# Sparse attention into a Swish MLP: batch 2's first transposes, batch 1's norms, and the later score and AV groups take other places in the order

## The chip, the cores and the metric

One core of a Trainium2 chip runs the whole kernel. The metric is device time in microseconds (us), the median of several runs. The engines of the core work side by side, each through its own list of instructions in order: TensorE (PE in the profile) does matmuls, VectorE (DVE) and ScalarE (ACT) do element-wise work, GpSimd (POOL) and SyncE (SP) here mostly send DMAs. An engine that reaches an instruction whose input is not ready waits, and so does all that is behind it on that engine.

## The reference

Four batches of eight heads, 768 tokens, head size 64. Each query sees the keys within 16 positions of it, and besides them 24 block summaries: the maximum of the keys, and the mean of the values, of each block of 32 tokens. The heads' outputs side by side are the 512 features of a token, and these go through a two-layer MLP with Swish.

```python
k_sum = k.reshape(B, H, nb, block, D).max(axis=3)
v_sum = v.reshape(B, H, nb, block, D).mean(axis=3)
scores_l = scale * np.matmul(q, k.transpose(0, 1, 3, 2))      # kept where |i - j| < 16
scores_s = scale * np.einsum('bhsd,bhnd->bhsn', q, k_sum) + np.log(block)
a = softmax over [scores_l | scores_s]
attn_out = np.matmul(a, concat([v, v_sum]))                   # -> x (3072 x 512)
h = x @ w_in                                                  # 512 -> 2048
out = (h * sigmoid(beta * h)) @ w_out                         # 2048 -> 512
```

## The kernel before, in words

The heads of a batch are taken two at a time, so a batch has four pairs, 0 to 3. For a pair:

- GpSimd loads v, k and q as bf16 (`load_next`, with lines 111, 118, 124 and 126). In the trace the loaded tiles are ve, k_nat and q_nat.
- `copy_v` (line 328) makes a second, shifted copy of v, vo, with two DMAs on SP. `cross` (lines 303 and 305) turns k and q by two transposing DMAs on SP, into kw and qt. For batch 0 and half of batch 1 TensorE turns them instead, and for two pairs of batch 1 ScalarE copies v.
- `max_k` (lines 311 and 313; `top_k`, line 293, in batch 1) takes the key maxima of the blocks on VectorE, and `rows_k` (lines 319 and 320) puts them beside the keys. `mean_v` (line 340 on TensorE, 347 on VectorE) and `rows_v` (line 353) do the same for the means of v.
- `scores` (line 438) is done for two pairs at once: 144 small matmuls in three groups, each followed by ScalarE's exponential (line 440). `mask` (line 447, VectorE) clears what is outside the window, one instruction for a pair.
- `av` (line 464) multiplies by v on TensorE, `norm` (lines 473 and 474, VectorE) divides by the sums and leaves x_nat, and `x_transpose` turns it into xT: by a transposing DMA on SP (line 483), or for batch 0 and pairs 2 and 3 of batch 1 by TensorE (line 488).

For a batch's MLP, 16 "h groups" (line 509 on TensorE, then ScalarE's Silu, line 516) make the hidden layer, and 24 "o parts" of four matmuls each (line 530) the output. Four o parts are 128 tokens: then ScalarE copies the result to o_sb, of which there are three buffers (line 550), and SP stores it (line 551). I number these stores 0 to 5 within a batch.

The order of all this is written out by hand. The loop over b (line 637) works on batch b's MLP and, in its gaps, on batch b+1's attention; I call its rounds stage 0, 1, 2 and 3. The MLP steps form the list `main`, with times in a planner's own unit: an h group counts 1.3, an o part 0.865, and `up` (20.8) is where the o parts begin. The attention steps are put into the list `side` by `at_time(t, ...)`, and each is issued just ahead of the first step of `main` whose time is not below t. So the numbers in the code are places in an order, the same for every engine's queue, and not times on the chip. In stage 0 an `open_gate` step lets GpSimd begin batch 2's loads; batch 3's loads are steps of stage 1. At the end of a stage come two steps of the next stage's MLP on three quarters of its input, which need xT of pairs 0, 1 and 2; the next stage then begins with the last quarter, pair 3.

Of the kernel before, what the change touches and what calls it, by code (L numbers as in the profile page):

```python
# [12 lines left out]
def kernel(  # L13
# [94 lines left out]
    def load_row(nm, b, g):  # L108
        t = qk_pool.tile([P, nch, 2, D], bf16, name=nm + "_nat", tag=nm + "_row")
        for h in range(2):  # L110
            nc.gpsimd.dma_start(out=t[:, :, h], in_=(k_row if nm == "k" else q_row)[b, g, :, h])  # L111
        nat[(nm, b, g)] = t

    def load_v(b, g, n=1):
        lo, hi = PC * g + 1, min(PC * (g + n) + 1, HC)
        rows = v[b].rearrange("h s d -> (h s) d")
        src = rows[lo * P - W:hi * P - W].rearrange("(c p) d -> p c d", p=P)
        nc.gpsimd.dma_start(out=ve_bufs[b % 2][:, lo:hi, 0:D], in_=src)  # L118

    def load_v_edge(b, last):  # L120
        ve = ve_bufs[b % 2]
        rows = v[b].rearrange("h s d -> (h s) d")
        if last:
            nc.gpsimd.dma_start(out=ve[0:W, HC, 0:D], in_=rows[H * S - W:H * S])
        else:
            nc.gpsimd.dma_start(out=ve[W:P, 0, 0:D], in_=rows[0:P - W])
# [370 lines left out]
    def h_group(u, i, ks=range(k1)):  # L497

        b, t0, w = units[u]
        nn = 2 // w  # L500
        if 0 in ks:
            if (i * nn) % (k2 // w) == 0:
                h_bufs[(u, i * nn * w // k2)] = moe_pool.tile([P, k2 // w, w * MG], bf16, name="h_sb", tag="h_sb", bufs=4)
            h_open[(u, i)] = ps.tile([P, 2, 512], f32, name="h_ps", tag="big", bufs=3)
        big = h_open[(u, i)]
        for j in range(2):
            ni, tok = (i, t0 + j * MG) if w == 2 else (2 * i + j, t0)
            for ki in ks:
                nc.tensor.matmul(big[:, j, 0:MG], w_in_sb[:, ki, ni * P:(ni + 1) * P], xT[b][:, ki, tok:tok + MG],  # L509
                                 start=(ki == 0), stop=(ki == k1 - 1))  # L510
        if k1 - 1 not in ks:
            return
        for j in range(nn):
            ni = i * nn + j
            hb = h_bufs[(u, ni * w // k2)][:, ni % (k2 // w)]
            nc.scalar.activation(out=hb.rearrange("p (k m) -> p k m", m=MG), in_=big[:, j:j + w, 0:MG],  # L516
                                 func=ACTF.Silu, scale=beta_sb[:, ni:ni + 1])
# [119 lines left out]
    for b in range(B):  # L637
        us = [u for u, z in enumerate(units) if z[0] == b]
        up = sum(NG[u] for u in us) * GT
        total = up + nch * 4 * OT  # L640
        nxt = b + 1 if b + 1 < B else None
        pairs = tuple(range(npair))
        side = []

        def at_time(t, f, *a):
            side.append((t, lambda: f(*a)))

        if b == 0:
            for g in pairs:
                t = 3.9 if g < 2 else 6.5  # L650
                at_time(0.6 + 1.3 * g, mask_half, g)
                at_time(0.6 + 1.3 * g, rows_v, 0, g, HM, nch)
                if g % 2 == 0:
                    at_time(t, av_pair, g)
                at_time(t, norm, (0, g, 1), HM)
                at_time(t + 2.6, x_transpose, (0, g, 1), HM, HM, "t", dve)
            at_time(7.0, fill_band, 0, HM)
            at_time(7.0, band_edge, False)
            for n in range(k2):
                at_time(up - 7.5 + 0.4 * n, scale_w_out, n)  # L660
        if nxt == 1:
            for g in pairs:
                if g < 2:
                    p = up - 9.0 + 4.5 * g
                    at_time(p, prep_k, 1, g, "t")
                    at_time(p, prep_q, 1, g, "t", dve)
                    at_time(p + 0.8, copy_v, 1, g)
                else:
                    p = (up + 6.1, up + 7.8)[g - 2]
                    at_time(up + 0.5, cross, 1, g)  # L670
                    at_time((up + 4.0, up + 6.1)[g - 2], copy_v, 1, g, 0, nch, act)
                at_time(p, top_k, 1, g)
                at_time(p, rows_k, 1, g)
            at_time(up + 3.4, mean_v, 1, pairs, "big")
            for g0, t, r, a, xt in ((0, up + 0.3, up + 3.4, up + 7.7, 0.1), (2, up + 12.9, up + 12.9, up + 17.2, 2.6)):
                at_time(t, scores, 1, g0)
                for f in (rows_v, mask):
                    for g in (g0, g0 + 1):
                        at_time(r, f, 1, g)
                for g in (g0, g0 + 1):  # L680
                    at_time(a, av, (1, g), 0, nch)
                for g in (g0, g0 + 1):
                    at_time(a, norm, (1, g), nch)
                    at_time(a + xt, x_transpose, (1, g), 0, nch, "big", dve)
        elif nxt is not None:
            for g in pairs:

                at_time(0.1 + 0.2 * g, copy_v, nxt, g)
                at_time(0.2 + 0.2 * g, cross, nxt, g)
                m = 3.9 + 3.9 * g if g < 2 else up + 1.0  # L690
                at_time(m, max_k, nxt, g)
                at_time(m, rows_k, nxt, g)
            at_time(14.0, mean_v, nxt, pairs)
            for g in pairs:
                at_time(14.1 + 1.0 * g, rows_v, nxt, g)
            for g0, t, a in ((0, up + 0.8, up + 5.9), (2, up + 9.0, up + 14.5)):
                at_time(t, scores, nxt, g0)
                for g in (g0, g0 + 1):
                    at_time(t, mask, nxt, g)
                    at_time(a, av, (nxt, g), 0, nch)  # L700
                for g in (g0, g0 + 1):
                    at_time(a, norm, (nxt, g), nch)
                    at_time(a, x_transpose, (nxt, g), 0, nch, "big", dve)
        if nxt is not None:
            if nxt + 1 < B:
                def load_next(b, g):
                    if g == 0:
                        nc.gpsimd.memset(ve_bufs[b % 2][SUM:P, 0:HC, D:VW], 1.0)
                        load_v_edge(b, False)
                    load_v(b, g)  # L710
                    if g == npair - 1:
                        load_v_edge(b, True)
                    load_row("k", b, g)
                    load_row("q", b, g)

                def open_gate():

                    nc.vector.memset(gate[:], 0.0)
                    nc.gpsimd.memset(gate[:], 0.0)

                if b == 0:
                    at_time(up + 6.0, open_gate)
                for g in pairs:
                    at_time(up + 6.0 + 0.01 * (g + 1) if b == 0 else 8.0 + 3.5 * g, load_next, nxt + 1, g)
        main = []
        for j, u in enumerate(us):
            for i in range(NG[u]):
                ks = range(k1 - 1, k1) if j == 0 and i < 2 else range(k1)
                main.append(((j * NG[u] + i) * GT, lambda u=u, i=i, ks=ks: h_group(u, i, ks)))
        for j, u in enumerate(us):  # L730
            n = units[u][2] * HM
            main += [(up + (4 * (j * n + ms) + p) * OT, lambda u=u, ms=ms, p=p: o_part(u, ms, p, 4)) for ms in range(n) for p in range(4)]
        if nxt is not None:
            main += [(total + i, lambda i=i: h_group(us[-1] + 1, i, range(k1 - 1))) for i in range(2)]
        side.sort(key=lambda z: z[0])
        for t, f in main:
            while side and side[0][0] <= t:
                side.pop(0)[1]()
            f()
        for _, f in side:  # L740
            f()
# [30 lines left out]
```

## Time and profile before

| | us |
|---|---|
| median of 3 runs (214.22 to 215.84) | 214.43 |
| the profiled execution, its own time | 214.58 |
| its span, first to last instruction | 212.9 |
| TensorE busy | 202.8 |
| ScalarE busy | 116.7 |
| VectorE busy | 87.8 |
| GpSimd busy | 66.8 |

TensorE's granted clock is 0.997 of full speed over the span. Busy times overlap, since the engines run side by side. The DMA engines are busy from the start to about 130 us, and much less after that.

How to read the rows that follow. A timeline row gives start, duration, engine, line, operation, what is written and read, and how many instructions were merged; in brackets stands how long the engine had been idle before, and what ended that. SPq is SP's queue, whose rows last as long as SP is occupied with sending. A DMA's "landing" is counted from the start of its sending until its data has arrived. A row of waits has the waiting work, what it waited for, and then the sum, the number and the longest. A row of the page's groups ends in busy us, mean ns of one, and idle time ahead of it. Matmuls overlap, so the mean duration of one is longer than its share of the busy time.

### The profile page before, as it was taken

Reading aid. Unit: us, or ns where it says so; the run is one execution under the profiler, and the core shown is the slowest. Engines: PE = TensorE matmul, PEld = TensorE weight load, DVE = VectorE, ACT = ScalarE, POOL = GpSimd, SP = SyncE. Lnnn points to the kernel's source line nnn. Section 1 sums busy time; section 2 is a strip of 40 time slices with the busy share of each in tenths; the row PEclk is TensorE's granted clock in tenths of the full one; section 3 lists DMA queues with packets and bytes.
Section 4 is the critical chain, followed back from the end, with each engine's and each line's share of the span. In section 5 each row is a group of like instructions: output and inputs, shape, how many; then the busy total and the mean of one; then the engine's idle time right before and its main releaser. Section 6 shows DMA issues by size and latency. Waiting matters only on the chain.

```text
span 212.9 us, 4838 instructions
## 1 busy us (share of the span) xinstructions
PE 202.8 (95%) x2005; PEld 113.6 (53%) x2024; DVE 87.8 (41%) x219; ACT 116.7 (55%) x159; POOL 66.8 (31%) x90
## 2 busy tenths in 40 slices
PE   7999999999989999999999799999999999999992
PEld 2656666655545565555455355555455565554452
DVE  4677891882795502164834005313834000002121
ACT  3799668889635186668161366668162476630000
POOL 7984344353399555555391000000000000000000
PEclk9999999999999999999999999999999999999998
DMA  6999999999999999999999999700153400001222
GB/s 174 174 156 188 205 204 206 186 179 168 155 156 188 235 192 169 158 123 161 144 155 145 199 229 180 139 3 0 64 161 98 127 0 3 0 2 59 89 89 62
DMA packets 93622, 28.34 MB, mean 133 GB/s; under 512 B 82256, under 2 KB 90656, under 8 KB 93600
## 3 DMA queue, kind: packets, MB, share of 16 engines
q0 software_dynamic: 63184, 13.24, 78.3%
q1 hardware_dynamic: 29968, 14.26, 35.8%
q10 hardware_dynamic: 448, 0.52, 0.7%
q8 instruction: 16, 0.26, 0.6%
q14 instruction: 6, 0.05, 0.1%
HBM read 27.27 MB, written 6.29 MB: 158 GB/s over the span
## 4 chain that ended last, share of the span: by engine, by line
PE 84%; DMA 9%; issue 2%; DVE 2%; ACT 1%; SPq 0%; POOL 0%; POOLq 0%
PE h_ps L509 39%; PE o_ps L530 33%; DMA xT<-x_nat 4%; DMA qt<-q_nat 3%; DMA q_run<-in_q_dram 3%; PE av_ps L464 2%; PE s_ps L438 2%; PE vm_ps L340 1%; PE px L488 1%; DVE x_nat L474 1%; PE pq L279 1%; PE pk L279 1%; PE s_ps L383 1%; PE av_ps L411 1%; PE s_ps L378 1%
## 5 line engine op out<-in xcount | busy, mean ns | idle before, releaser
L509 PE MATMUL h_ps<-xT,w_in_sb 128*128 128x384 bf16 x512 | 85.9, 326 | 1.6 <-DMA xT<-x_nat 1.5
L530 PE MATMUL o_ps<-w_out_sb,h_sb 128*128 128x512 bf16 (+2 forms) x383 | 82.9, 370 | 2.0 <-issue 1.6
L516 ACT ACTIVATE h_sb<-h_ps,beta_sb 128x768 bf16<-128x768 f32 (+1 forms) x80 | 59.3, 772 | 25.1 <-PE h_ps L509 25.0
L509 PEld LDWEIGHTS <-w_in_sb 128*128 128x128 bf16 x512 | 49.2, 98 | 35.0 <-issue 2.1
L530 PEld LDWEIGHTS <-h_sb 128*128 128x128 bf16 x400 | 37.5, 98 | 41.6
L550 ACT COPY o_sb<-o_ps 128x512 f32<-128x512 f32 x18 | 10.7, 592 | 33.2 <-PE o_ps L530 16.8
L111 POOL DMA_DIRECT2D k_nat<-in_k_dram x20 | 16.8, 842 | 15.5 <-DMA ve<-in_v_dram 5.7
L440 ACT ACTIVATE attn<-s_ps 128x1024 bf16<-128x1024 f32 x18 | 17.2, 1024 | 7.2 <-PE s_ps L438 7.1
L111 POOL DMA_DIRECT2D q_nat<-in_q_dram x20 | 16.8, 847 | 9.9 <-DMA ve<-in_v_dram 6.5
L550 DVE COPY o_sb<-o_ps 128x512 f32<-128x512 f32 x5 | 3.5, 692 | 39.5 <-PE o_ps L530 39.5
L447 DVE TENSOR_TENSOR attn<-attn,band 128x1536 bf16<-128x1536 bf16 x12 | 11.2, 957 | 13.9 <-ACT attn L440 13.8
L118 POOL DMA_DIRECT2D ve<-in_v_dram x12 | 14.3, 1191 | 7.0 <-DMA w_in_sb<-in_moe_w_in_dram 2.7
L474 DVE TENSOR_TENSOR x_nat<-av_ps,r 128x768 bf16<-128x768 f32 (+1 forms) x20 | 16.0, 798 | 0.7
L311 DVE TENSOR_TENSOR half<-kw 128x384 bf16<-128x384 bf16 x8 | 2.8, 355 | 28.2 <-DMA kw<-k_nat 28.2
L293 DVE TENSOR_REDUCE km<-kw 128x24 bf16<-128x768 bf16 x8 | 7.6, 948 | 2.4 <-DMA kw<-k_nat 1.3
L473 DVE RECIPROCAL r<-av_ps 128x12 f32<-128x12 f32 (+1 forms) x20 | 4.2, 212 | 8.3 <-PE av_ps L464 7.5
L464 PEld LDWEIGHTS <-attn 128*64 128x64 bf16 x336 | 6.0, 111 | 3.0 <-issue 2.4
L298 DVE COPY qt<-pq 128x768 bf16<-128x768 bf16 x5 | 4.8, 958 | 5.8 <-PE pq L279 5.8
L464 PE MATMUL av_ps<-vo,attn 128*64 128x65 bf16 x168 | 6.9, 196 | 0.0
L353 DVE COPY ve<-vm 32x780 bf16<-32x780 bf16 x12 | 4.9, 408 | 4.7 <-DMA vo<-ve 4.4
L464 PE MATMUL av_ps<-ve,attn 128*64 128x65 bf16 x168 | 6.8, 196 | 0.0
L438 PEld LDWEIGHTS <-kw 64*128 64x128 bf16 x288 | 4.7, 95 | 3.4 <-issue 2.0
(92 smaller groups left out, 142.4 us busy)
## 6 DMA issues: line engine op xcount, KB each, us to landing
out_dram<-o_sb SPq DMA_DIRECT2D x23, 256.0 KB, 4.4
w_out_sb<-in_moe_w_out_dram POOLq DMA_DIRECT2D x4, 512.0 KB, 17.5
k_nat<-in_k_dram POOLq DMA_DIRECT2D x20, 96.0 KB, 10.6
q_nat<-in_q_dram POOLq DMA_DIRECT2D x20, 96.0 KB, 10.7
w_in_sb<-in_moe_w_in_dram POOLq DMA_DIRECT2D x3, 512.0 KB, 14.4
ve<-in_v_dram POOLq DMA_DIRECT2D x6, 192.0 KB, 10.8
vo<-ve SPq DMA_DIRECT2D x10, 97.5 KB, 6.6
ve<-in_v_dram POOLq DMA_DIRECT2D x2, 384.0 KB, 12.8
```

The costliest lines, as they stand in the source:

```text
L111: nc.gpsimd.dma_start(out=t[:, :, h], in_=(k_row if nm == "k" else q_row)[b, g, :, h])
L118: nc.gpsimd.dma_start(out=ve_bufs[b % 2][:, lo:hi, 0:D], in_=src)
L293: nc.vector.tensor_reduce(out=km_of[g], in_=keys_of(b, g).rearrange("p (n f) -> p n f", f=block), op=ALU.max, axis=mybir.AxisListType.X)
L438: nc.tensor.matmul(sv[:, h, c], kw_of(b, g)[lo:lo + D, par, m, :], qt_bufs[g][lo:lo + D, m, par], start=True, stop=True)
L440: nc.scalar.activation(out=flat[:, j * n:(j + 1) * n].rearrange("p c h f -> p h c f"), in_=sv, func=ACTF.Exp, scale=scale)
L447: nc.vector.tensor_mul(out=a, in0=a, in1=band.rearrange("p r m h f -> p (r m h f)"))
L464: nc.tensor.matmul(ov[par * QT:(par + 1) * QT, h, m], a[:, par, m, h], t[:, PC * g + nch * h + m0 + m], start=True, stop=True)
L474: nc.vector.tensor_mul(out=x.rearrange("p m h d -> p h m d"), in0=ov[:, :, :, 0:D], in1=r[:, :, :, None].to_broadcast([P, 2, n, D]))
L509: nc.tensor.matmul(big[:, j, 0:MG], w_in_sb[:, ki, ni * P:(ni + 1) * P], xT[b][:, ki, tok:tok + MG], start=(ki == 0), stop=(ki == k1 - 1))
L516: nc.scalar.activation(out=hb.rearrange("p (k m) -> p k m", m=MG), in_=big[:, j:j + w, 0:MG], func=ACTF.Silu, scale=beta_sb[:, ni:ni + 1])
L530: nc.tensor.matmul(o_ps[:, c0:c1], h_bufs[(u, ni * w // k2)][:, ni % (k2 // w), ms * P:(ms + 1) * P], w_out_sb[:, ni, c0:c1], start=(ni == ...
L550: (nc.scalar.copy if u + 1 < len(units) else nc.vector.tensor_copy)(out=o_sb[:], in_=o_ps[:])
```

## The change

Nothing is computed otherwise; steps take other places in the list. With times in the planner's unit:

- Stage 0: `copy_v` and `cross` of batch 2's pairs 0 and 1, which stood first in stage 1, are issued at up+17.4 and up+19.1, which is ahead of o parts 21 and 23 (counted from 0), and so on SP between store 4 and store 5. Pairs 2 and 3 stay first in stage 1.
- Stage 0: `top_k` and `rows_k` of batch 1's pair 2 go from up+6.1 to up+7.8, that is from ahead of `norm` of pairs 0 and 1 to behind them. `av` and `norm` of its pairs 2 and 3 go from up+17.2 to up+16.4, from ahead of o part 20 to ahead of o part 19, and their `x_transpose` from part 23 to part 22.
- Stages 1 and 2: `max_k` and `rows_k` of pair 2 go from up+1.0 to 11.7 and of pair 3 from up+1.0 to 18.0, so from behind both masks of pairs 0 and 1 to ahead of them; pair 2's are now also ahead of `mean_v`, pair 3's behind the last `rows_v`.
- Stages 1 and 2: `av` and what follows it of pairs 0 and 1 go from ahead of o part 7 to ahead of part 6; `scores` of pairs 2 and 3 from part 11 to part 9; their `av`, `norm` and `x_transpose` from part 17 to part 14. On SP the last two x transposes thereby come ahead of store 3 instead of behind it.

```diff
                 else:
-                    p = (up + 6.1, up + 7.8)[g - 2]
+                    p = up + 7.8
...
-            for g0, t, r, a, xt in ((0, up + 0.3, up + 3.4, up + 7.7, 0.1), (2, up + 12.9, up + 12.9, up + 17.2, 2.6)):
+            for g0, t, r, a, xt in ((0, up + 0.3, up + 3.4, up + 7.7, 0.1), (2, up + 12.9, up + 12.9, up + 16.4, 2.6)):
...
         elif nxt is not None:
             for g in pairs:
 
-                at_time(0.1 + 0.2 * g, copy_v, nxt, g)
-                at_time(0.2 + 0.2 * g, cross, nxt, g)
-                m = 3.9 + 3.9 * g if g < 2 else up + 1.0
+                if nxt > 2 or g > 1:
+                    at_time(0.1 + 0.2 * g, copy_v, nxt, g)
+                    at_time(0.2 + 0.2 * g, cross, nxt, g)
+                m = 3.9 + 3.9 * g if g < 3 else 18.0
...
-            for g0, t, a in ((0, up + 0.8, up + 5.9), (2, up + 9.0, up + 14.5)):
+            for g0, t, a in ((0, up + 0.8, up + 5.1), (2, up + 7.7, up + 12.0)):
...
                 if b == 0:
                     at_time(up + 6.0, open_gate)
+                    for g in range(2):
+                        at_time(up + 17.4 + 1.7 * g, copy_v, 2, g)
+                        at_time(up + 17.4 + 1.7 * g, cross, 2, g)
```

## The prediction

> **What bounds the kernel now.** I read the page first, then TensorE's waits, the chain of work in order of time, and last the timelines of TensorE, VectorE and SP around the places that the diff touches.
>
> ```profile
> PE 202.8 (95%) x2005; PEld 113.6 (53%) x2024; DVE 87.8 (41%) x219; ACT 116.7 (55%) x159; POOL 66.8 (31%) x90
> ...
> L509 PE MATMUL h_ps<-xT,w_in_sb 128*128 128x384 bf16 x512 | 85.9, 326 | 1.6 <-DMA xT<-x_nat 1.5
> L530 PE MATMUL o_ps<-w_out_sb,h_sb 128*128 128x512 bf16 (+2 forms) x383 | 82.9, 370 | 2.0 <-issue 1.6
> ...
> L550 ACT COPY o_sb<-o_ps 128x512 f32<-128x512 f32 x18 | 10.7, 592 | 33.2 <-PE o_ps L530 16.8
> ```
>
> ```profile
> PE h_ps L509 <- DMA xT<-x_nat: 1.5, 1, 1.5
> PE s_ps L438 <- DMA qt<-q_nat: 0.8, 1, 0.8
> ```
>
> TensorE is busy for 95% of the span, and no matmul is added or removed. So only its idle time can change the end: the two waits above, the start before its real work begins, and the last few us. The rows give two prices. A matmul of the first layer costs 85.9 / 512 = 0.168 us of TensorE's time, one of the second 82.9 / 383 = 0.216 us, so an "o part" of four matmuls is 0.87 us.
>
> The largest wait stands at the end of the stage that works on batch 1's tokens and prepares batch 2 (stage 1, some 74 to 123 us; stage 0 is the one before it, stage 2 the one behind). From the chain, then from TensorE's timeline:
>
> ```profile
> 68.46 0.89 PE av_ps L464 x48
> ...
> 101.96 0.88 PE av_ps L464 x48
> ...
> 115.60 7.61 DMA xT<-x_nat
> ...
> 149.85 0.88 PE av_ps L464 x48
> ...
> 167.41 20.80 PE h_ps L509 x128
> ```
>
> ```profile
> 119.36 0.49 PE L509 MATMUL h_ps<-xT,w_in_sb 128*128 128x384 bf16 x2
> 121.39 4.78 PE L509 MATMUL h_ps<-xT,w_in_sb 128*128 128x384 bf16 x27 [1.54 <-DMA xT<-x_nat]
> ```
>
> After two matmuls from 119.36 the third could start at 119.70; it starts at 121.39, when pair 2's transposed x lands: 1.7 us lost. Ten more end at 121.39 + 1.68 = 123.07, and pair 3's x, landing at 115.60 + 7.61 = 123.21, lets the next go: 0.2 us (rounded up). Together **1.9 us**, all that the change can win in this place. Stage 2 ends in 167.41 with no DMA before it in the chain: nothing to win there.
>
> **The change part by part.**
>
> *Stage 0.* Batch 1's norms go ahead of pair 2's maxima, and the AV of its pairs 2 and 3 stands one o part earlier.
>
> ```profile
> 65.03 1.83 DVE L447 TENSOR_TENSOR attn<-attn,band 128x1536 bf16<-128x1536 bf16 x2
> ```
>
> VectorE does the same work, begins it with the norms instead of waiting for pair 2's keys, and is later nowhere. Batch 1's x leaves no earlier, as SP is still sending the stores ahead of it. The AV, at 68.46 - 0.87 = 67.6, stands behind masks that end at 66.9. The 0.8 us wait for the queries is untouched. Zero.
>
> *The later AV groups move up* (AV of pairs 2 and 3: three o parts earlier in stages 1 and 2). In stage 1 the norms behind them, and with them SP's two x transposes, come 3 x 0.87 = 2.6 us earlier, on SP's queue now ahead of one output store. Landings at 121.39 and 123.2 would become 118.8 and 120.6; needed at 119.7 and 121.4. If nothing else moved, the 1.9 us would be gone with 0.8 us to spare. In stage 2 the same move wins nothing.
>
> *The AV of pairs 0 and 1* stands one o part earlier, at 101.96 - 0.87 = 101.1 in stage 1; its second half (pair 1) starts 0.44 us later, 101.55. These read what VectorE has masked:
>
> ```profile
> 99.22 1.87 DVE L447 TENSOR_TENSOR attn<-attn,band 128x1536 bf16<-128x1536 bf16 x2 [0.67 <-ACT attn L440]
> 101.01 0.35 DVE L311 TENSOR_TENSOR half<-kw 128x384 bf16<-128x384 bf16 x1
> ...
> 102.35 0.35 DVE L311 TENSOR_TENSOR half<-kw 128x384 bf16<-128x384 bf16 x1
> ```
>
> ```profile
> 147.11 1.88 DVE L447 TENSOR_TENSOR attn<-attn,band 128x1536 bf16<-128x1536 bf16 x2 [7.75 <-ACT attn L440]
> ```
>
> The two masks end at 100.2 and 101.1, so with VectorE's order unchanged both AV halves would find their input ready, the second with 0.45 us of cover. In stage 2 (147.11 and 149.85) cover is the same, and VectorE idles 7.75 us ahead of the masks.
>
> *The key maxima of pairs 2 and 3 move ahead of the masks* (max_k and rows_k, from up+1.0 to 11.7 and 18.0). One set takes 102.35 - 101.01 = 1.34 us. Before, both sets ran behind the masks and asked for keys long landed. Now VectorE, which works in order, reaches pair 3's maxima first, and both masks are queued behind them. What counts is when pair 3's transposed keys land:
>
> ```profile
> 74.77 1.14 SPq L328 DMA_DIRECT2D vo<-ve  x2
> ...
> 92.32 2.17 SPq L303 DMA_TRANSPOSE kw<-k_nat  x1
> ```
>
> ```profile
> L303 SPq DMA_TRANSPOSE kw<-k_nat x4: 1284/2081/2168, 76.1 to 92.3; - x4
> ...
> DMA to landing us min/median/max: 7.5/9.1/9.1
> ```
>
> The second fence has batch 2's four key transposes, the first sent at 76.1, the last at 92.3. Today pair 3's land at 92.32 + 9.1 = 101.4, behind both masks. The move is free only if the keys land by 101.55 - 2 x 0.935 (masks) - 1.34 = **98.3**, that is 3.1 us earlier. Each us beyond that is a us of TensorE.
>
> *Pairs 0 and 1 of batch 2 among the stores of stage 0.* Eight DMAs (per pair two v copies, one key and one query transpose) go on SP ahead of the last store. SP reaches them when store 4 is out. That store's last part now follows the AV: 67.6 + 0.89 + 0.87 = 69.4, then the copy (0.59) and the store's issue (about as long, an estimate by the v copies' 1.14 / 2), so 70.6 instead of 74.8: 4.2 us earlier. Store 5 stands behind the eight, to about 80; its buffer, one of three, is asked for by the third copy of the next stage, long after: nothing. But the transposes share the DMA engines with GpSimd's loads of the later pairs, and pair 3's keys must be loaded before they are transposed:
>
> ```profile
> L111 POOL DMA_DIRECT2D k_nat<-in_k_dram x1: 821/821/821, 78.4 to 78.4; - x1
> ...
> DMA to landing us min/median/max: 10.3/10.3/10.3
> ```
>
> ```profile
> q0 software_dynamic: 7574, 0.95, 149.1%
> q1 hardware_dynamic: 977, 1.22, 40.9%
> ```
>
> ```profile
> q0 software_dynamic: 4590, 0.57, 105.5%
> q1 hardware_dynamic: 3417, 1.06, 79.1%
> ```
>
> The last two fences are the DMA queues' packets (their count comes first) at 70 to 80 us and at 80 to 90 us; q0 carries GpSimd's loads, q1 SP's transfers. While SP's transposes run, the loads fall from 757 to 459 packets per us. 4.2 us more of that cost the loads 4.2 x 298 = 1250 packets, or 1250 / 459 = 2.7 us. Pair 3's keys, today in at 78.4 + 10.3 = 88.7, come at 91.4; SP is free by then, so its transpose goes out at 91.5, not at 92.3 - 4.2 = 88.1. With today's 9.1 us it lands at **100.6**. Bounds: loads undisturbed and the 7.5 us of the quickest of the four give 88.9 + 7.5 = 96.4; loads late by the whole 4.2 us give 93.0 + 9.1 = 102.1. I take 100.6, since 9.1 us is both the median and the slowest of the four, beside the same loads. VectorE then ends pair 1's mask at 100.6 + 1.34 + 1.87 = 103.8, and the AV that could run at 101.55 waits **2.3 us** (0 to 3.8).
>
> The Trainium skill, "DMA: Bandwidth & Descriptors", section "Queues, rings and completion order", says that each DMA engine takes turns between the queues that have work, a packet at a time. By that rule, with equal turns, the loads would get 400 of the 800 packets per us of the second stretch and lose 4.2 x 357 / 400 = 3.7 us, which makes the wait 3.3 us and the kernel 1 us slower than my sum. The trace's 4590 to 3417 is near equal turns, but nearer the loads' side, so I stay with the row.
>
> *Pair 2's maxima* now stand ahead of the v means on VectorE. Pair 2's keys are sent ahead of pair 3's and land ahead of them, so whatever waits there is through when pair 3's maxima wait; the v means' PSUM buffer is asked for again only by the second group of o parts. Nothing of its own. *The scores of pairs 2 and 3*, two o parts earlier, come behind the new wait, at 101.55 + 2.3 + 0.44 + 3 x 0.87 = 106.9, and so after pair 3's queries, which SP sends right behind its keys: nothing.
>
> *Sum*, against the profiled execution's own 214.58 us: - 1.9 + 2.3 = 214.98. That execution is 0.15 above the median of 214.43, so I predict **214.8**: the gain at the stage's end is spent at its middle.
>
> **Rivals.**
>
> *Slower.* The load delay compounds: each of GpSimd's loads waits for an earlier one to land, so a delay is passed on, pair 3's keys come past 93 and the transpose lands at 103 to 104. The wait is 4.7 to 5.7 us and the time 217.2 to 218.2. It decides from a landing at 102.4 on (wait 4.1, time 216.6). For it, GpSimd's own waits:
>
> ```profile
> POOL k_nat L111 <- DMA ve<-in_v_dram: 5.7, 3, 3.6
> ```
>
> Its key loads waited three times for a v load to land, 5.7 us in all. Against: SP goes quiet earlier, and the loads then run at the faster rate.
>
> *Faster.* The keys land by 98.3: SP's queue, shorter by two pairs, moves each transfer in less than 9.1 us, and loads catch up while SP waits. Then only the 1.9 us counts: 212.5. For it: the quickest of the four transposes, at 7.5 us. Against: SP cannot send before the load is in, and pair 3's two v copies still stand ahead of it.
>
> *Nothing moves.* x still lands late because the loads end later, and the masks are not held: 214.4. Against: 0.8 us of spare and one store fewer ahead.
>
> **How the numbers follow.** Partly or wholly cancelled (wait 1 to 4 us, 213.5 to 216.5): 0.63, with 214.8 in it. Faster, wait under 1 us, 212.4 to 213.5: 0.19. Slower, over 216.6: 0.13. Nothing moves: 0.05. About 1% (2.1 us) is what a measurement of this kernel can tell from no change. Over 1% faster needs all of the 1.9 us and a piece of the 0.8 us wait besides: 0.03. Over 1% slower is the slower rival: 0.13. Within 1%: 0.84. The range, 212.5 to 216.9, leaves out the slower rival and the very edge of the faster one.
>
> **What would show it.** Right: TensorE no longer waits at the end of stage 1, and has a new idle of about 2 us ahead of the AV near 101 us, with VectorE idle just before pair 3's maxima, released by the key transpose. Pair 3's key load lands some 3 us later than today. Wrong: no idle there (the keys came in time), or the wait for x still stands at the end of the stage, or a new wait in stage 2, where I expect none.

## The result, and the profile after

The changed kernel takes 215.37 us (median of 22 runs, 213.98 to 218.28), the kernel before 214.31 beside it; the ratio is 1.0052 (95% interval 1.0028 to 1.0076). The forecast was 214.8 us against 214.43, a ratio of 1.002. So the sign of the sum was right and the size nearly, but in the profile the loss does not stand where the sum had it.

The profiled execution took 217.66 us and is longer than the median, because in it TensorE's clock fell as shown below; the ratio leaves the longest executions out.

From the page of the changed kernel, and then its waits of TensorE:

```profile
span 215.9 us, 4859 instructions
...
PE 207.4 (96%) x2024; PEld 114.6 (53%) x2024; DVE 87.5 (41%) x219; ACT 116.9 (54%) x159; POOL 67.2 (31%) x90
...
PEclk9999999999999999769999999999999999999999
```

```profile
PE vm_ps L340 <- DMA ve<-in_v_dram: 3.0, 2, 2.3
PE w_ps L560 <- DVE warm L156: 1.3, 1, 1.3
```

The wait for x at the end of stage 1 is gone, as forecast. There is no wait ahead of the AV. Instead a wait stands where the prediction had none: at `mean_v`, which takes the block means of v and needs the v of all four pairs. The clock row shows two slices of the 40, between 86 and 97 us, in which TensorE was not granted its full speed. TensorE's timeline around it, and the windows of 2 us (their last columns are the granted clock, the DMA share and GB/s):

```profile
86.60 0.24 PE L340 MATMUL vm_ps<-ve,A_avg 128*32 128x130 bf16 x3
89.12 0.84 PE L340 MATMUL vm_ps<-ve,A_avg 128*32 128x130 bf16 x24 [2.28 <-DMA ve<-in_v_dram]
90.69 0.27 PE L340 MATMUL vm_ps<-ve,A_avg 128*32 128x130 bf16 x1 [0.73 <-DMA ve<-in_v_dram]
```

```profile
88.00:90.00 2.00, 0.84 (x24) 0.65 (x24) 0.00 (x0) 0.00 (x0) 1.39 (x2) 0.73 2.44 115
90.00:92.00 2.00, 1.31 (x5) 0.58 (x5) 0.00 (x0) 0.00 (x0) 1.27 (x3) 0.50 1.33 130
92.00:94.00 2.00, 2.00 (x8) 0.91 (x6) 0.52 (x2) 0.34 (x1) 1.88 (x3) 0.50 1.59 103
94.00:96.00 2.00, 2.00 (x8) 1.00 (x7) 1.86 (x7) 0.57 (x1) 2.00 (x3) 0.56 2.30 162
```

From the chain of work, the same place in the kernel before and then in the changed one:

```profile
87.87 0.52 PE vm_ps L340 x24
88.39 6.61 PE h_ps L509 x40
```

```profile
90.95 8.98 PE h_ps L509 x40
...
106.03 0.88 PE av_ps L464 x48
```

The means took 0.52 us from start to end, and now 90.95 - 86.60 = 4.35: 3.8 us lost. The forty matmuls behind them took 6.61 us and now 8.98, at half clock for much of it: 2.4 us more. Against that stand the 1.9 us won at the end of the stage, and the 1.2 us by which this execution is ahead when it comes to the means (86.60 against 87.80 us in TensorE's timelines): 0.2 us of these are from the start of the program, and the largest part is the wait for the queries in stage 0, which is missing in this execution (it is back, with 0.8 us, in an experiment below that has the same stage 0, so it comes and goes). 3.8 + 2.4 - 1.9 - 1.2 = 3.1, and the spans differ by 3.0.

What TensorE waited for are GpSimd's loads of pair 3's v (line 118) and of the last 16 rows (line 124). First the two in the kernel before, then in the changed one:

```profile
L118 POOL DMA_DIRECT2D ve<-in_v_dram x1: 1052/1052/1052, 73.4 to 73.4; - x1
...
DMA to landing us min/median/max: 13.8/13.8/13.8
```

```profile
L124 POOL DMA_DIRECT2D ve<-in_v_dram x1: 524/524/524, 74.4 to 74.4; - x1
...
DMA to landing us min/median/max: 12.9/12.9/12.9
```

```profile
L118 POOL DMA_DIRECT2D ve<-in_v_dram x1: 1052/1052/1052, 74.8 to 74.8; - x1
...
DMA to landing us min/median/max: 14.2/14.2/14.2
```

```profile
L124 POOL DMA_DIRECT2D ve<-in_v_dram x1: 524/524/524, 76.4 to 76.4; - x1
...
DMA to landing us min/median/max: 14.3/14.3/14.3
```

Before, they land at 87.2 and 87.3, half a us ahead of the means at 87.87. Now they land at 89.0 and 90.7. A cover of half a us was spent by a delay of two to three.

### The profile page after: what moved, and what is told of

The parts are those of the page before. It is cut to its first block, busy times and chain, and to the rows that moved or that the text cites. A ratio compares the mean times of both kernels' runs of the same rounds, so it can differ in the third digit from the quotient of the medians.

```text
span 215.9 us, 4859 instructions
## 1 busy us (share of the span) xinstructions
PE 207.4 (96%) x2024; PEld 114.6 (53%) x2024; DVE 87.5 (41%) x219; ACT 116.9 (54%) x159; POOL 67.2 (31%) x90
## 4 chain that ended last, share of the span: by engine, by line
PE 56%; DMA 31%; POOL 7%; issue 4%; DVE 0%; POOLq 0%; DVEq 0%
PE o_ps L530 29%; PE h_ps L509 23%; DMA ve<-in_v_dram 19%; DMA k_run<-in_k_dram 7%; DMA k_nat<-in_k_dram 5%; PE av_ps L464 2%; POOL q_nat L111 2%; PE s_ps L438 1%; POOL ve L118 1%; POOL k_nat L111 1%; POOL q_run L106 1%; POOL k_run L106 1%; POOL ve L126 0%; PE vm_ps L340 0%; POOL near L171 0%
## 5 line engine op out<-in xcount | busy, mean ns | idle before, releaser
L509 PE MATMUL h_ps<-xT,w_in_sb 128*128 128x384 bf16 x512 | 87.8, 333 | 0.0
L530 PE MATMUL o_ps<-w_out_sb,h_sb 128*128 128x512 bf16 (+2 forms) x400 | 86.0, 371 | 0.0
L509 PEld LDWEIGHTS <-w_in_sb 128*128 128x128 bf16 x512 | 50.2, 99 | 35.4 <-issue 3.6
L340 PE MATMUL vm_ps<-ve,A_avg 128*32 128x130 bf16 x112 | 3.7, 241 | 3.0 <-DMA ve<-in_v_dram 3.0
L399 ACT ACTIVATE attn<-s_ps 128x768 bf16<-128x768 f32 x8 | 6.0, 808 | 0.7 <-PE s_ps L383 0.6
```

The costliest lines, as they stand in the source:

```text
L399: nc.scalar.activation(out=out, in_=src, func=ACTF.Exp, scale=scale)
L530: nc.tensor.matmul(o_ps[:, c0:c1], h_bufs[(u, ni * w // k2)][:, ni % (k2 // w), ms * P:(ms + 1) * P], w_out_sb[:, ni, c0:c1], start=(ni == ...
```

## The experiments

Theory M (means): the early transposes delay the loads, and the first to meet that is TensorE at the means, with the clock at half behind a wait that is long enough. Rival K (keys), the forecast's own: what costs time is the masks queued behind pair 3's maxima. Both can be true, one hiding the other. Diffs are against the changed kernel unless said; a ratio is to the kernel before, timed beside each run.

**The means three h groups later.**

```diff
-            at_time(14.0, mean_v, nxt, pairs)
+            at_time(18.1 if nxt == 2 else 14.0, mean_v, nxt, pairs)
...
-                at_time(14.1 + 1.0 * g, rows_v, nxt, g)
+                at_time(18.11 + 0.01 * g if nxt == 2 else 14.1 + 1.0 * g, rows_v, nxt, g)
...
-                m = 3.9 + 3.9 * g if g < 3 else 18.0
+                m = 3.9 + 3.9 * g if g < 3 else 18.15 if nxt == 2 else 18.0
```

> The changed kernel with stage 1's mean_v, its rows_v and pair 3's maxima three h groups later (some 3.9 us), so that TensorE asks for pair 3's v at about 91.8 us, behind the 90.6 us at which its last piece landed in the changed kernel's profile. Theory M (the change lost its time where TensorE's mean_v waited 3.0 us for pair 3's v, with the clock at half behind it): no wait at the means, clock near 1.00 in all runs, and the forecast's own wait appears in its place, about 1.5 us ahead of the AV near 101 us, because the keys still land at some 99.9; time 213.5 to 214.3. Rival K (the forecast: only the masks behind pair 3's maxima cost time, the means cost nothing of their own): the time stays at 215 or more, as the maxima's place before the masks is the same.

Measured: 215.11 us, ratio 1.0016 (0.9974 to 1.0057), so no clear gain. By the time alone this is what rival K expects, and theory M's 213.5 to 214.3 is missed. But the wait has changed its place. TensorE's only long wait, and VectorE's rows ahead of the masks:

```profile
PE av_ps L464 <- DVE attn L447: 5.1, 1, 5.1
```

```profile
102.59 0.36 DVE L311 TENSOR_TENSOR half<-kw 128x384 bf16<-128x384 bf16 x1 [3.62 <-DMA kw<-k_nat]
...
104.09 1.82 DVE L447 TENSOR_TENSOR attn<-attn,band 128x1536 bf16<-128x1536 bf16 x2
```

Pair 3's maxima wait 3.62 us for the transposed keys, and the masks stand behind them: the forecast's mechanism, with 5.1 us (in the profiled execution) where I expected 1.5 at this place. This is the longest of the run's twelve executions. The keys landed at 102.6 here and at 99.9 in the changed kernel, so this size differs between executions. The clock fell to 0.50 here too, at 102.5 us within this wait, and stayed there until 109.3 us.

**The means late, and pair 3's maxima behind the masks again.** As before, with

```diff
-                m = 3.9 + 3.9 * g if g < 3 else 18.0
+                m = 3.9 + 3.9 * g if g < 3 else up + 1.0 if nxt == 2 else 18.0
```

> As the run before, and besides pair 3's maxima of batch 2 go back behind the masks, where they were. Theory M with the forecast's second wait: neither the means nor the masks wait any more, the x wait at the end of the stage is gone as well, so the whole 1.9 us is won: 212.4. If the maxima's place does not matter, the time is that of the run before (within 0.3 us).

Measured: 212.29 us, ratio 0.9904 (0.9872 to 0.9936). The rows of TensorE's waits:

```profile
PE w_ps L560 <- DVE warm L156: 1.3, 1, 1.3
PE s_ps L438 <- DMA qt<-q_nat: 0.8, 1, 0.8
```

None is left in stage 1, and the time falls by 2.0 us, the 1.9 that the forecast put on the x wait. So both waits were real: with the means out of the way the masks wait, and with both out of the way nothing does. Run again on another chip:

> The kernel with stage 1's means, its copies and pair 3's maxima late, once more on this chip, to see whether its gain holds: 212.0 to 212.6, a ratio of 0.988 to 0.994. If the first result was a favourable draw of the loads' timing: above 213.

Measured: 212.0 us, ratio 0.9889 (0.9833 to 0.9945). It holds, and beats both kernels.

**No early transposes, the rest as changed.**

```diff
-                if nxt > 2 or g > 1:
-                    at_time(0.1 + 0.2 * g, copy_v, nxt, g)
-                    at_time(0.2 + 0.2 * g, cross, nxt, g)
+                at_time(0.1 + 0.2 * g, copy_v, nxt, g)
+                at_time(0.2 + 0.2 * g, cross, nxt, g)
...
-                    for g in range(2):
-                        at_time(up + 17.4 + 1.7 * g, copy_v, 2, g)
-                        at_time(up + 17.4 + 1.7 * g, cross, 2, g)
```

> The changed kernel with pairs 0 and 1 of batch 2 copied and transposed first in stage 1 again, as before the change; all else changed. The loads are then those of the kernel before, so by theory M there is no wait at the means. Pair 3's keys land at 101.4 as before, and the maxima hold the masks: a wait of 104.6 - 101.55 = 3.1 us at the AV, 1.9 us won at the end, 215.5. If the early transposes were the whole loss and the maxima harmless: 212.4.

Measured: 216.11 us, ratio 1.0059 (1.0031 to 1.0086). No wait at the means, but

```profile
PE av_ps L464 <- DVE attn L447: 2.3, 2, 2.1
```

The masks queued behind pair 3's maxima cost, without the early transposes, as much as the change as a whole. But it is not the forecast's mechanism alone. VectorE's rows:

```profile
94.34 0.36 DVE L311 TENSOR_TENSOR half<-kw 128x384 bf16<-128x384 bf16 x1 [4.90 <-DMA kw<-k_nat]
...
99.91 0.36 DVE L311 TENSOR_TENSOR half<-kw 128x384 bf16<-128x384 bf16 x1
...
101.26 1.82 DVE L447 TENSOR_TENSOR attn<-attn,band 128x1536 bf16<-128x1536 bf16 x2
```

VectorE waited for pair 2's keys, until 94.34, and then worked without a break; pair 3's keys were in at 99.6 (91.05 + 8.6), not at the 101.4 expected, and its maxima waited for nothing. So the masks are late by what pair 2's keys held up, and by the 1.35 us that pair 3's maxima take ahead of them. Had pair 2's keys come earlier, pair 3's, at 99.6, would have held the masks nearly as long. The clock was at 0.50 again, from 102.6 to 106.0 us, behind an idle of 2.1 us:

```profile
104.00:106.00 2.00, 2.00 (x9) 0.73 (x6) 1.31 (x3) 0.00 (x0) 1.98 (x3) 0.50 2.02 213
```

**The early transposes alone**, on the kernel before:

```diff
-                at_time(0.1 + 0.2 * g, copy_v, nxt, g)
-                at_time(0.2 + 0.2 * g, cross, nxt, g)
+                if nxt > 2 or g > 1:
+                    at_time(0.1 + 0.2 * g, copy_v, nxt, g)
+                    at_time(0.2 + 0.2 * g, cross, nxt, g)
...
                     at_time(up + 6.0, open_gate)
+                    for g in range(2):
+                        at_time(up + 17.4 + 1.7 * g, copy_v, 2, g)
+                        at_time(up + 17.4 + 1.7 * g, cross, 2, g)
```

> The kernel before with one edit: pairs 0 and 1 of batch 2 copied and transposed among the stores of stage 0. No AV, score or maxima step moves. Theory M (the early transposes delay the loads, and TensorE meets that at the means): pair 3's v lands 2 to 4 us later than its 87.4 us, TensorE waits 2 to 3 us at the means at about 88 us, in part of the runs with the clock at half behind it; what the end of the stage loses to x stays or shrinks: 215.5 to 217. Rival K (only the masks behind the maxima matter): the masks stand ahead of pair 3's maxima here, so nothing is lost: 214 to 214.7.

Measured: 215.19 us, ratio 1.0031 (0.9996 to 1.0067), between the two expectations. The wait is there, but smaller than expected, and the time is not clear of no change:

```profile
PE vm_ps L340 <- DMA ve<-in_v_dram: 1.2, 1, 1.2
...
PE h_ps L509 <- DMA xT<-x_nat: 0.5, 1, 0.5
```

The wait at the means takes the place of part of the wait for x (1.5 before, 0.5 now). The direction is theory M's; by itself this run would not have shown it.

**The later score and AV groups alone**: no early transposes (diff above), and the maxima of pairs 2 and 3 where they were before the change, in stages 1 and 2:

```diff
-                m = 3.9 + 3.9 * g if g < 3 else 18.0
+                m = 3.9 + 3.9 * g if g < 2 else up + 1.0
```

> Only the later scores and AV groups stand earlier, and batch 1's norms and AV as in the change; the early transposes and the maxima's places are as before the change. By the forecast's sum this has the gain without any of the losses: no wait at the means, at the masks or for x at the end of stage 1: 214.3 - 1.9 = 212.4. If the x wait is only moved (x lands late whatever the order, since the DMA engines are loaded until 125 us): 213.5 to 214.3.

Measured: 214.61 us, ratio 0.9998 (0.9977 to 1.0019). Both expectations were missed. The wait for x is gone, but a new one stands in its place, once in stage 1 and once in stage 2:

```profile
PE s_ps L438 <- DVE x_nat L474: 1.4, 2, 0.7
```

The two sets of maxima behind the masks keep VectorE from the norms, and the scores of pairs 2 and 3, now two o parts earlier, ask for a PSUM buffer that the norms have not yet read out. Moving maxima ahead of the masks thus pays for the earlier scores, a part of the change that my sum had priced at nothing. 1.4 us given back leaves 0.5 us of the 1.9; the median does not show it, though the lower end of the interval, 0.9977, would just hold it.

**One part undone: pair 3's maxima behind the masks**, the means early:

```diff
-                m = 3.9 + 3.9 * g if g < 3 else 18.0
+                m = 3.9 + 3.9 * g if g < 3 else up + 1.0 if nxt == 2 else 18.0
```

> The changed kernel with one part undone: pair 3's maxima of batch 2 stand behind the masks again. Theory M: the wait at the means is as in the changed kernel (some 3 us, in part of the runs with the clock at half behind it) and hides the masks' wait anyway, so nothing is won: 214.8 to 215.6. Rival K: the whole loss is gone: 212.4.

Measured: 214.2 us, ratio 0.9987 (0.9955 to 1.0018). The wait at the means is there (1.2 us in the profile), and the gain at the end of the stage is spent by it and smaller waits. Theory M expected that nothing is won against the changed kernel, and this is missed: the ratios, 0.9987 and 1.0052, have intervals that do not touch. The means stand ahead of pair 3's maxima in the order, so it is not likely that the maxima's place changes the wait at the means. The masks' wait, hidden in the changed kernel's profile, then most likely costs time in other executions of it; no profile shows one of these.

With four runs the two waits can be weighed against each other. The ratios:

| | pair 3's maxima ahead of the masks | behind the masks |
|---|---|---|
| means early | 1.0052 (the change) | 0.9987 |
| means late | 1.0016 | 0.9904 |

With the means late, the maxima's place costs 1.0016 - 0.9904 = 1.1%, or 2.4 us. With the maxima behind the masks, the early means cost 0.9987 - 0.9904 = 0.8%, or 1.8 us. Both together cost 1.5%, or 3.2 us, so about 1 us of the one is hidden by the other. Each ratio is known to 0.2 to 0.4%, so these sizes are good to about 1 us.

**Pair 3's maxima behind the masks, and no early transposes.** The diff above together with that of "No early transposes".

> The changed kernel with two parts undone: pairs 0 and 1 of batch 2 are copied and transposed first in stage 1 again, and pair 3's maxima of batch 2 stand behind the masks again. Pair 2's maxima and the score and AV groups stay as changed, the means stay where they were. If the early transposes are no help and both losses are gone: no wait in stage 1 except at most 0.3 us, 212.3, as the run with means and maxima late. If the early transposes are needed for pair 2's maxima (its keys land at 95 instead of 92 us, the masks come late by up to 1 us): 212.8 to 213.5.

Measured: 213.5 us, ratio 0.9953 (0.992 to 0.9986), at the edge of the second of the two cases. Now pair 2's keys are late: VectorE's row, with its wait, and TensorE's:

```profile
95.74 0.36 DVE L311 TENSOR_TENSOR half<-kw 128x384 bf16<-128x384 bf16 x1 [5.82 <-DMA kw<-k_nat]
```

```profile
PE av_ps L464 <- DVE attn L447: 1.4, 2, 1.1
```

With the early transposes and the means late, these keys landed at 91.6. So the early transposes are worth some 1 us (ratios 0.9953 and 0.9904, whose intervals overlap a little), once what they delay is out of the way.

**Pair 3's v loaded earlier**, in one DMA with pair 2's, and the last 16 rows right behind it; pair 3's maxima behind the masks (not in the diff), the means early:

```diff
-                    load_v(b, g)
-                    if g == npair - 1:
+                    if b != 2 or g < 2:
+                        load_v(b, g)
+                    elif g == 2:
+                        load_v(b, 2, 2)
+                    if g == (2 if b == 2 else npair - 1):
                         load_v_edge(b, True)
```

> The changed kernel with pair 3's maxima behind the masks, the means where the change has them, and batch 2's v of pair 3 loaded together with pair 2's, so ahead of pair 2's k and q on GpSimd's queue. Theory M: what TensorE waited for at the means was this load; it now lands several us before 86 us, so the means do not wait, and nothing else is held: 212.3, as with means and maxima late. If the wait at the means has another cause (the small last piece, the PSUM buffer, the order on TensorE): 214.2, as with the maxima late alone.

Measured: 212.86 us, ratio 0.9904 (0.9868 to 0.9939). The load:

```profile
L118 POOL DMA_DIRECT2D ve<-in_v_dram x1: 1482/1482/1482, 66.5 to 66.5; - x1
...
DMA to landing us min/median/max: 18.4/18.4/18.4
```

It lands at 84.9, the wait at the means is gone without moving the means, and the gain is back. That settles the load as the cause of the wait at the means.

**The wait filled**, the changed kernel with idle work in it:

```diff
+            if nxt == 2:
+                at_time(13.95, keep_warm, 10)
             at_time(14.0, mean_v, nxt, pairs)
```

> The changed kernel with ten more matmuls of a constant tile (10 x 0.216 us = 2.2 us, their result is not used) ahead of stage 1's means, so that TensorE is busy for most of the wait for pair 3's v. Theory M: the wait is filled and not shortened, so a run costs what the changed kernel's runs with a clock of 0.998 or more cost (213.98 to 215.43, middle 214.9), and no run shows a clock below 0.995: 214.5 to 215.3, with a smaller spread than 213.98 to 218.28. If the fall of the clock has nothing to do with TensorE's idle: half of the runs still lie at 215.7 and above, and the median is at 216 or more. Rival K: the fill adds up to 2.2 us where no wait stands, 216.5 to 217.5.

Measured: 214.85 us, 213.99 to 216.5, ratio 1.0037 (1.0005 to 1.0068). Its profile has no wait in stage 1, 2.2 us of fill instead, and

```profile
88.00:92.00 4.00, 4.00 (x48) 2.11 (x47) 0.00 (x0) 0.81 (x2) 1.64 (x2) 1.00 1.91 122
92.00:96.00 4.00, 4.00 (x27) 2.44 (x25) 3.70 (x9) 2.80 (x4) 3.73 (x5) 1.00 3.02 129
```

The granted clock stays at 1.00 where it was at 0.50, and the highest of the times falls from 218.28 to 216.5. The mean clocks of all executions say the same: of the changed kernel's 22, nine have 0.983 to 0.990 and the others 0.996 or more; here all twelve have 0.996 or more, as theory M expected. So the fall of the clock belongs to TensorE's idle. They also bound its price, of which a longer wait may be a part: the changed kernel's 13 executions with a clock of 0.996 or more have a median of 214.8 us, as here, 0.5 us above the kernel before, and the other nine took 215.68 us or more.

## Why the prediction came out as it did, point by point

- *x at the end of stage 1*: right. The wait is gone in every profile with the later groups moved, and the version without the other losses wins 2.0 us where 1.9 us was forecast.
- *The loads' delay*: right in kind. Pair 3's keys were to land 2.7 us late, at 91.4. In the changed kernel:

```profile
L111 POOL DMA_DIRECT2D k_nat<-in_k_dram x1: 821/821/821, 82.0 to 82.0; - x1
...
DMA to landing us min/median/max: 10.4/10.4/10.4
```

  That is 92.4, against 88.7 before: 3.7 us. The estimate by equal turns, from the Trainium skill's "DMA: Bandwidth & Descriptors", section "Queues, rings and completion order", was 3.7 us, and this execution agrees with it. But one execution can't decide between that rule and the row that I kept to: in the profiles of the six other runs with early transposes and the same order of loads, the keys landed between 91.0 us (means and maxima late, run again) and 94.6 us (maxima behind the masks). The transposed keys were forecast for 100.6; they landed at 99.9, as VectorE's rows in the changed kernel show:

```profile
99.87 0.36 DVE L311 TENSOR_TENSOR half<-kw 128x384 bf16<-128x384 bf16 x1 [1.45 <-DMA kw<-k_nat]
...
104.16 1.87 DVE L447 TENSOR_TENSOR attn<-attn,band 128x1536 bf16<-128x1536 bf16 x2 [2.85 <-ACT attn L440]
```

- *Who meets the delay first*: wrong, and this is the step of the sum that failed: "But the transposes share the DMA engines with GpSimd's loads of the later pairs, and pair 3's keys must be loaded before they are transposed". I followed the keys only. The same queue brings pair 3's v, two steps ahead of the keys, and TensorE asks for it at the means, at 87.87 with 0.5 us of cover. That wait came 15 us ahead of the one I priced. It moved all of stage 1 back, so that the keys at 99.9 were early enough: in this execution the masks (104.16) waited for ScalarE, and TensorE did not wait at the AV. By the four ratios, the loss that the sum left out is 1.8 us alone and 0.8 us on top of the forecast one.
- *The masks behind pair 3's maxima*, 2.3 us (0 to 3.8): right as a mechanism. The run with the means late has it in full, with 5.1 us in its profile, and by the four ratios its price there is 2.4 us. With the early transposes, the AV waits 0 to 0.3 us where the maxima are back behind the masks. In the changed kernel's profile it costs nothing, being hidden. ("Keys long landed" was misread for pair 3: its keys were in at 101.4, 1 us before the second set of maxima began.)
- *The clock*: not in the sum. The Trainium skill, "TensorE: Matmul & The Clock Gate", "Part 1: The HAM clock gate", has the clock halved after an idle window of some 3.4 us; here an idle of 2.1 us was enough (no early transposes), in the changed kernel's profile the clock fell 2.1 us after the start of the idle of 2.3 us, and an idle of 1.2 us was not enough.
- *Pair 2's maxima, and the scores*: "nothing" was wrong for both. The maxima's move is what lets the norms free the scores' PSUM buffers, and pair 2's maxima are what the early transposes help. Without these, what waits at pair 2's maxima is not through when pair 3's come: VectorE had no pause from 94.34 us until the masks.
- *Stage 0 and stage 2*: right, the changed kernel has no new wait there. The 0.8 us wait of stage 0 comes and goes between executions.

The time came out inside the range since the forecast loss is about as large as forecast, and about half of the loss that was left out is hidden by it, or hides it, as in the profile. That the missing term moved the time so little is luck.

## What to carry to other kernels

When transfers are sent earlier on a loaded DMA system, list every load that they delay and, for each, every engine that reads it, with the cover it has: the first to run out of cover pays, and it can hide part of what those behind it pay. A moved step is best judged after the new wait is taken away by a small move of its own: here two late steps turned a loss of 0.5% into a gain of 1%. And on TensorE a wait of two or three us can cost one or two us more in clock.

## What the runs showed of the hardware

Idles of 2.1 and 2.3 us were enough to halve TensorE's granted clock. By windows of 0.25 and 0.5 us it stayed at half for 3.4 us without the early transposes (102.6 to 106.0 us), and for 6.8 us in the changed kernel (88.9 to 95.8 us) and with the means late (102.5 to 109.3 us). A transposing DMA for one pair's keys landed after 2.7 us in stage 2 of the kernel before, with no loads left, and after 7.5 to 9.1 us beside the loads of stage 1; where SP's transfers ran, the loads' packets fell by 40%. Loads sent in the same order landed up to 3 us apart from one execution to the next (the last 16 rows of v at 87.8 us with means and maxima late, at 90.7 us in the changed kernel), and the same program order up to the means made waits there of 1.2 us (maxima behind the masks) and 3.0 us (the changed kernel).
